# A float64-weight MoE kernel: one VectorE merge per weight block with its low bits from ScalarE, and late attention scores whose odd heads swap their two halves

## The chip, the cores and the metric

The kernel runs on one core of one Trainium2 chip. The metric is device time in microseconds (us) of one execution, the median of a few runs; lower is better. TensorE is PE in the profile (PEld its weight loads), VectorE is DVE, ScalarE is ACT, GpSimd is POOL, and SyncE (SP) issues every DMA.

## The reference

Three stages follow each other; batch 4, 8 heads of 48, 768 positions, model width 384.

```python
def _attn_ref(r, k, v, w, u):            # a recurrent state per head, decayed by w at every position
    for t in range(S):
        cur = np.einsum('bhd,bhe->bhde', u[None] * kt, vt)
        y[:, :, t] = np.einsum('bhd,bhde->bhe', rt, state + cur)
        state = wt[:, :, :, None] * state + np.einsum('bhd,bhe->bhde', kt, vt)

def _moe_ref(x, w_gate, w_val, w_out, rms_g):      # 3072 tokens, 384 -> 1536 -> 384
    xn = x / np.sqrt(np.mean(x * x, axis=-1, keepdims=True) + 1e-06) * rms_g
    g = xn @ w_gate
    return g * (1.0 / (1.0 + np.exp(-g))) * (xn @ w_val) @ w_out

def _moe2_ref(x, w_in, w_out, s, b):               # 3072 tokens, 384 -> 2048 -> 384
    r = np.maximum(x @ w_in, 0.0)
    return (s * (r * r) + b) @ w_out
```

The weights of both MoE stages are float64 and are handed over as 64-bit patterns.

## The kernel before, in words

**Work and order.** The 768 positions are 6 chunks of 128, and a chunk of all 4 batches is 512 columns. A pair `jb` (0 to 23) is one chunk of one batch. For each pair `attention` (L335) makes the decays, the scores, the output and the new state; `attention_x` normalises and turns the result; the first MoE (12 blocks f a chunk) and the second (16 blocks a chunk) follow. Every matmul of the MoE parts is done in three passes (high weight with high input, high with low, low with high; L629 to L631, L646). Chunks 0 and 1 are done in two parts, since not all weights are there yet, and partly in halves of 256 columns.

Nothing is issued in the order in which it is written. `op` hands each step to `Plan` with a due time and a cost per engine; `Plan.issue` walks through time with these costs and puts each step into its engine's queue, and `FIRST_OPS` (L53) replaces the due time of some 100 steps, found by their number. Where the planner sees TensorE idle, it puts in a filler, a matmul on zeros (`idle`, L820), which reads and writes nothing that is used. A step that may run on two engines (`BOTH`) goes to the one that is free first. The queues are in order: an engine that waits holds up all that stands behind.

**Weights** (`weights`, L576). A block of float64 weights comes in by DMA (`raw`, 768 or 384 numbers a row) and becomes a float32 pattern `pat` in three VectorE passes: L599 moves the high word three bits up, L603 merges the sign and exponent bits of the high word, L605 merges the top three bits of the low word. ScalarE then rounds `pat` to the high part of `w` (L610), and VectorE or, in the second MoE, either VectorE or GpSimd subtracts it for the low part (L620). There are 40 such pieces: 24 in the first MoE (12 of 768 and 12 of 384) and 16 of 768 in the second. Two `raw` and two `pat` buffers take turns.

**Scores** (`scores`, L399 to L405). Heads lie in two groups of 64 rows (`p`), four heads `h` each. From pair 4 on the scores of a head are done in two halves: keys 0 to 63 against 128 queries into the lower 64 output partitions, and keys 64 to 127 against the last 64 queries into the upper 64. So one quarter of the array streams 128 columns and the other 64, for each of the four heads. ScalarE copies the scores to `a` (L319), GpSimd zeroes what lies in the future with one select of 128x512 per `p` (L426), and TensorE multiplies by `v` in `sums` (L454) behind the products with the state (L445).

**Decays.** r and k are multiplied by running products of w (`re`, `ke`): on VectorE up to pair 11, from pair 12 on VectorE or GpSimd.

**Check.** Beside the second MoE, VectorE tests that all weights lie where the bit moves are right (`check_weight`, L760); otherwise a slow path, which does not run here, would do everything again.

## Time and profile before

| what | value |
|---|---|
| median of 3 runs | 967.43 us (966.9 to 967.6) |
| the profiled execution, own time | 967.64 us |
| its span, first to last instruction | 965.9 us |
| around the span | 1.7 us |
| busy share of the span: PE, DVE, ACT, POOL | 99%, 66%, 39%, 17% |
| granted TensorE clock, mean | 0.997 |

A line of a group of instructions gives source line, engine, operation, out<-in, shapes and count, then busy time, the mean of one in ns, the engine's idle time just before them and what ended most of it. In a timeline the first two numbers are start and length in us, and x32 says that 32 equal instructions were merged. Lengths of neighbours overlap a little, since an instruction starts before its predecessor has drained; the step from one start to the next is what an engine spends. A busy TensorE includes the fillers (L822).

### The profile page before, as it was taken

The page shows a single profiled execution, that of the slowest core. Times are in us where ns is not written, and L with a number is a line of the kernel's source. Part 1 is how long each engine was busy: PE and PEld are TensorE (multiplying, and loading weights), DVE is VectorE, ACT ScalarE, POOL GpSimd, SP SyncE. Part 2 cuts the span into 40 slices and gives each one's busy share as a digit, 9 for nine tenths or more (in the row PEclk, how much of TensorE's full clock was granted, in tenths as well). Part 3 has the DMA queues.
Part 4 walks back from the last instruction along what each step waited for, and adds up shares of the span by engine and source line. Part 5 has one row for each costly group of instructions (what it writes and reads, how often), then busy time and mean ns, then how long its engine had stood idle before and what let it go on. Part 6 is the DMA issues. An engine that isn't in the chain of part 4 may idle for free.

```text
span 965.9 us, 16522 instructions
## 1 busy us (share of the span) xinstructions
PE 952.9 (99%) x6585; PEld 788.7 (82%) x6589; DVE 635.2 (66%) x1051; ACT 378.8 (39%) x782; POOL 162.6 (17%) x211
## 2 busy tenths in 40 slices
PE   9999999999999999999999999999999999999996
PEld 5898998888888887888888878888888888888885
DVE  8999898547445445532588799987777874433332
ACT  4756545534323332332343353343433433433333
POOL 1212211255433323110025440000000000000000
PEclk9999999999999999999999999999999999999998
DMA  8655554245434443222466465553354530000001
GB/s 259 196 169 158 173 158 140 83 112 149 101 84 118 122 93 95 69 69 61 122 225 206 150 212 178 158 194 113 114 182 132 178 117 1 33 0 1 34 1 36
DMA packets 74422, 115.79 MB, mean 120 GB/s; under 512 B 28384, under 2 KB 48096, under 8 KB 74336
## 3 DMA queue, kind: packets, MB, share of 16 engines
q1 hardware_dynamic: 74336, 114.65, 39.6%
q8 instruction: 53, 0.87, 0.4%
q14 instruction: 33, 0.27, 0.1%
HBM read 99.16 MB, written 15.47 MB: 119 GB/s over the span
## 4 chain that ended last, share of the span: by engine, by line
PE 91%; DVE 5%; DMA 2%; ACT 1%; issue 1%; SPq 0%; POOL 0%; DVEq 0%
PE b L646 48%; PE b L629 12%; PE b L630 11%; PE b L631 11%; PE b L454 2%; PE b L404 2%; PE b L445 1%; DMA raw<-in_w 1%; DMA in<-in_rkw 1%; DVE pat L605 1%; DVE pat L603 1%; PE b L408 0%; PE b L822 0%; PE b L469 0%; DVE pat L599 0%
## 5 line engine op out<-in xcount | busy, mean ns | idle before, releaser
L646 PE MATMUL b<-xh,w 128*128 128x512 f32 (+1 forms) x1566 | 485.2, 374 | 0.9 <-DVE sg L316 0.6
L646 PEld LDWEIGHTS b<-xh,w 128*128 128x128 f32 x1566 | 287.7, 188 | 55.6 <-issue 1.9
L646 PE MATMUL b<-xl,w 128*128 128x512 f32 (+1 forms) x783 | 291.1, 372 | 0.0
L629 PE MATMUL b<-hh,w 128*128 128x512 f32 (+1 forms) x537 | 205.0, 382 | 1.1 <-ACT in L681 0.7
L630 PE MATMUL b<-hl,w 128*128 128x512 f32 (+1 forms) x537 | 202.5, 377 | 1.4 <-DVE hl L316 1.4
L631 PE MATMUL b<-hh,w 128*128 128x512 f32 (+1 forms) x537 | 202.1, 376 | 0.0
L319 ACT ACTIVATE sg<-b 128x512 f32<-128x512 f32 (+1 forms) x179 | 102.6, 573 | 249.1 <-PE b L646 245.0
L646 PEld LDWEIGHTS b<-xl,w 128*128 128x128 f32 x783 | 147.3, 188 | 25.4
L717 DVE SCALAR_TENSOR_TENSOR sg<-sg,cs,b 128x512 f32<-128x512 f32 (+1 forms) x97 | 71.9, 741 | 90.0 <-ACT sg L319 89.8
L630 PEld LDWEIGHTS b<-hl,w 128*128 128x128 f32 x537 | 101.0, 188 | 20.2 <-DVE hl L316 2.5
L629 PEld LDWEIGHTS b<-hh,w 128*128 128x128 f32 x537 | 101.0, 188 | 20.1 <-ACT in L681 0.9
L631 PEld LDWEIGHTS b<-hh,w 128*128 128x128 f32 x537 | 101.0, 188 | 18.5
L720 DVE SCALAR_TENSOR_TENSOR hl<-sg,cs,hh 128x512 fp32r<-128x512 f32 (+1 forms) x97 | 73.0, 753 | 43.4 <-ACT hh L319 43.2
L319 ACT ACTIVATE hh<-sg,cs 128x512 fp32r<-128x512 f32 (+1 forms) x97 | 70.1, 722 | 75.9 <-DVE sg L717 71.4
L319 ACT ACTIVATE hh<-sg 128x512 fp32r<-128x512 f32 (+1 forms) x82 | 47.6, 581 | 114.9 <-DVE sg L316 109.5
L316 DVE TENSOR_TENSOR sg<-b,sg 128x512 f32<-128x512 f32 (+1 forms) x82 | 51.0, 623 | 62.1 <-PE b L646 52.9
L316 DVE TENSOR_TENSOR hl<-sg,hh 128x512 fp32r<-128x512 f32 (+1 forms) x82 | 57.3, 698 | 18.2 <-ACT hh L319 17.5
L620 POOL TENSOR_TENSOR w<-pat,w 128x384 fp32r<-128x384 f32 x29 | 39.8, 1394 | 67.2 <-ACT w L610 67.2
L610 ACT ACTIVATE w<-pat 128x384 fp32r<-128x384 f32 x68 | 32.8, 520 | 37.5 <-DVE pat L605 37.3
L316 DVE TENSOR_TENSOR ys<-b,av 128x192 f32<-128x192 f32 x40 | 13.8, 351 | 47.8 <-PE b L454 47.8
L426 POOL TENSOR_SCALAR_AFFINE_SELECT a<-a 128x512 f32<-128x512 f32 x38 | 29.6, 796 | 85.7 <-ACT a L319 85.4
L603 DVE SCALAR_TENSOR_TENSOR pat<-raw,pat 128x768 uint32<-128x768 uint32 (+1 forms) x40 | 35.7, 894 | 0.0
(128 smaller groups left out, 843.4 us busy)
## 6 DMA issues: line engine op xcount, KB each, us to landing
raw<-in_w SPq DMA_DIRECT2D x56, 768.0 KB, 4.4
in<-in_rkw SPq DMA_DIRECT2D x24, 448.0 KB, 4.6
raw<-in_w SPq DMA_DIRECT2D x24, 384.0 KB, 3.6
n<-in_nat SPq DMA_DIRECT2D x18, 384.0 KB, 3.4
in<-in_rkw SPq DMA_DIRECT2D x24, 226.6 KB, 3.0
x2d<-o SPq DMA_DIRECT2D x21, 256.0 KB, 2.4
a<-in_rkw SPq DMA_DIRECT2D x24, 224.0 KB, 2.9
v<-in_nat SPq DMA_DIRECT2D x24, 192.0 KB, 4.0
```

The lines of the kernel that those rows point to most:

```text
L316: op(when, {e: cost[e] for e in engines}, lambda e: E[e].tensor_tensor(dst, a, b, f), reads, writes, port)
L319: op(when, {"act": act(n)}, lambda e: nc.scalar.activation(dst, src, func, **kw), reads, writes)
L426: op(t, {"pool": 0.60}, lambda e, s=A[p]: nc.gpsimd.affine_select(out=AT[s], in_=AT[s], compare_op=ALU.is_gt, fill=0.0, base=0, pattern=[[ ...
L603: op(t, {"dve": vec2(N)}, lambda e, word=word, pat=pat: nc.vector.scalar_tensor_tensor(pat(), word(1), 0xC0000000, pat(), ALU.bitwise_and, ...
L610: op(t, {"act": act(DM)}, lambda e, c=c, s=s, pat=pat: nc.scalar.activation(W[s][:, 0], pat(c).bitcast(F32), AF.Copy), [("pat", pi)], [("w ...
L620: op(t, {"dve": vec2(DM)} if ph == 0 else {"dve": vec2(DM), "pool": gps(DM)}, lambda e, c=c, s=s, pat=pat: E[e].tensor_tensor(W[s][:, 1], ...
L629: nc.tensor.matmul(dst, wt[:, 0, cols], xh, start=first, stop=False, skip_group_check=True)
L630: nc.tensor.matmul(dst, wt[:, 0, cols], xl, start=False, stop=False, skip_group_check=True)
L631: nc.tensor.matmul(dst, wt[:, 1, cols], xh, start=False, stop=last, skip_group_check=True)
L646: nc.tensor.matmul(dst, W[s][:, w, kk * 128:(kk + 1) * 128], xx[x][:, kk, sl], start=first and j == kk == 0, stop=last and kk == KD - 1 an ...
L717: op(t, {"dve": vec2(n)}, lambda e: nc.vector.scalar_tensor_tensor(sg, sg, s_col, p, ALU.mult, ALU.mult), [("ps", i)], [("sg", q)], False)
L720: op(t, {"dve": vec2(n)}, lambda e: nc.vector.scalar_tensor_tensor(hl, sg, b_col, hh.bitcast(F32), ALU.add, ALU.subtract), [("sg", q), ("h ...
```

## The change

**Weights.** Of the three VectorE passes two remain: the first now makes a constant with the sign bit (L616 after the change), the last shifts the high word by three and merges it with an exclusive or (L628). The three low bits are written between them by ScalarE: it reads one byte of each float64, scales it by 1/32 and writes it as the lowest byte of `pat` (L624). This needs weights under 2.0, and the check changes accordingly (a minimum in place of a masked product).

**Late pairs** (12 to 23). In odd heads the two halves go to the other half of the output partitions, so that each quarter of the array streams 128 columns for two heads and 64 for the other two. The rows of `a` of these heads are then swapped, so their `v` is loaded once more with its halves swapped (`vs`, two DMAs of 48 KB a pair in pieces of 384 bytes), and GpSimd's one select becomes three smaller ones per `p`. The products of r and k with their decays are on VectorE alone.

**Order.** The table `FIRST_OPS` is another one (its numbers count the new steps), so all queues are ordered anew. One line of it stands for all.

```diff
-TD, LATE = 3, 60
+TD, LATE, EVEN = 3, 60, 12
 FIRST_OPS = {
-    0: 281.6, 22: 529.2, 37: 729.3, 38: 985.1, 39: 488.5, 46: 298.9, 57: 804.2, 58: 733.2, 64: 673.4, 75: -711.3,
...
+    0: 36.2, 10: 196.1, 29: 1237.4, 37: 2075.4, 38: 1931, 39: -101.4, 41: -1180.2, 42: 822.5, 44: -295.5, 46: 2565.9,
...
+    VS = tiles(2, "vs", [128, HP, D])
-        ke, re, ne = (DVE, DVE, DVE) if jb < EARLY else (BOTH, BOTH, BOTH)
+        ke, re, ne = (DVE, DVE, DVE) if jb < EARLY else (DVE, DVE, BOTH)
+        if even:
+            for z in (0, 64):
+                dma(tl[3], VS[q][z:z + 64].rearrange("p (g x) d -> p g (x d)", g=2),
+                    nat[jb, 64 - z:128 - z, 0:DM].rearrange("t (g o m) -> t g o m", g=2, o=2)[:, :, 1],
+                    64 * 4 * D * 4, (), [("vs", q, z)])
+                    to = slice(64 - c0, C - c0) if even and h % 2 else cols
-                        nc.tensor.matmul(sc[p][cols, h, c0:], k[rows, h, cols], r[rows, h, c0:],
+                        nc.tensor.matmul(sc[p][to, h, c0:], k[rows, h, cols], r[rows, h, c0:],
-            op(t, {"pool": 0.60}, lambda e, s=A[p]: nc.gpsimd.affine_select(
-                out=AT[s], in_=AT[s], compare_op=ALU.is_gt, fill=0.0, base=0, pattern=[[0, HP], [1, C]],
-                channel_multiplier=-1), (), [("a", A[p])])
+            pairs = AT[A[p]].rearrange("p (g o) t -> p g o t", o=2)
+            keep(t, pairs[:, :, 0], 0.37, 0, 2)
+            keep(t, pairs[0:64, :, 1], 0.37, -64, 2)
+            keep(t, pairs[64:128, :, 1, 0:64], 0.25, 0, 2)
+                    vj = VS[q][:, j // 4 * 2 + p] if even and h % 2 else v[:, j, :]
-                    nc.vector.tensor_scalar(pat(), m, 3, 0x3FFFFFFF, ALU.logical_shift_left, ALU.bitwise_and)
+                    nc.vector.tensor_scalar(pat(), m, 0x80000000, 0xC0000000, ALU.bitwise_and, ALU.bitwise_xor)
-            op(t, {"dve": vec2(N)}, lambda e, word=word, pat=pat: nc.vector.scalar_tensor_tensor(
-                pat(), word(1), 0xC0000000, pat(), ALU.bitwise_and, ALU.bitwise_or), [("raw", ri)], [("pat", pi)])
-            op(t, {"dve": vec2(N)}, lambda e, word=word, pat=pat: nc.vector.scalar_tensor_tensor(
-                pat(), word(0), 29, pat(), ALU.logical_shift_right, ALU.bitwise_or), [("raw", ri)], [("pat", pi)])
+                op(t, {"act": act(N)}, lambda e, raw=raw, pat=pat: nc.scalar.activation(
+                    pat().bitcast(U8).rearrange("p (n four) -> p n four", four=4)[:, :, 0],
+                    raw.bitcast(U8).rearrange("p (n eight) -> p n eight", eight=8)[:, :, 3],
+                    AF.Copy, scale=1.0 / 32.0, bias=-31.0 / 64.0), [("raw", ri)], [("pat", pi)])
+                op(t, {"dve": vec2(N)}, lambda e, word=word, pat=pat: nc.vector.scalar_tensor_tensor(
+                    pat(), word(1), 3, pat(), ALU.logical_shift_left, ALU.bitwise_xor), [("raw", ri)], [("pat", pi)])
```

How the queues change is shown at three places. The numbers behind the names tell buffers apart; they are shifted by two after the change, since two tiles were added.

First place: TensorE, just after the first MoE matmuls have begun, around the turning of the fourth pair's output (L563, L580 after the change: `b<-cs,l`). Before:

```order
L822 LDWEIGHTS zero_115
L822 MATMUL b_157<-zero_115 128x256
L563 MATMUL b_160<-cs_63,l_109 128x128 x3
L822 LDWEIGHTS zero_115
L822 MATMUL b_157<-zero_115 128x256
L646 MATMUL b_157<-xh_116,w_79 128x256
L646 MATMUL b_157<-xl_118,w_79 128x256
```

After the change:

```order
L669 MATMUL b_158<-xl_118,w_81 128x256
L669 MATMUL b_158<-xh_116,w_81 128x256
L580 MATMUL b_162<-cs_63,l_109 128x128 x3
L652 MATMUL b_160<-hh_122,w_77 128x256
L653 MATMUL b_160<-hl_124,w_77 128x256
L654 MATMUL b_160<-hh_122,w_77 128x256
L652 MATMUL b_161<-hh_122,w_77 128x256
```

The fillers here are gone, and the turn stands behind the third weight column `w_81` where it stood behind the first part of `w_79`. In the whole queue 15 fillers of 256 columns become 3, and of the fillers of 512 columns 46 become 44 (20 of them at the very start in both).

Second place: VectorE, the first block of weights, among the first two pairs (`a_136`, `a_137`, `a_138`, `l_110`: their masked scores). Before:

```order
L599 TENSOR_SCALAR pat_114<-raw_112 128x384
L599 TENSOR_SCALAR pat_113<-raw_111 128x768
L603 SCALAR_TENSOR_TENSOR pat_114<-raw_112,pat_114 128x384
L316 TENSOR_TENSOR n_132<-in_128 112x512
L605 SCALAR_TENSOR_TENSOR pat_114<-raw_112,pat_114 128x384
L603 SCALAR_TENSOR_TENSOR pat_113<-raw_111,pat_113 128x768
L316 TENSOR_TENSOR l_110<-b_162,mk_153 128x512
L605 SCALAR_TENSOR_TENSOR pat_113<-raw_111,pat_113 128x768
```

After the change:

```order
L616 TENSOR_SCALAR pat_114<-raw_112 128x384
L368 RECIPROCAL rg_70<-l_105 112x4x8
L317 TENSOR_TENSOR in_129<-in_129,l_105 112x512
L317 TENSOR_TENSOR a_138<-b_163,mk_155 128x512
L317 TENSOR_TENSOR a_139<-b_164,mk_155 128x512
L370 SCALAR_TENSOR_TENSOR l_106<-in_129,rg_70 112x516
L317 TENSOR_TENSOR st_71<-b_161,pm_146 112x192
L317 TENSOR_TENSOR in_129<-in_129,l_106 112x512
L616 TENSOR_SCALAR pat_113<-raw_111 128x768
L628 SCALAR_TENSOR_TENSOR pat_114<-raw_112,pat_114 128x384
L317 TENSOR_TENSOR n_134<-in_128 112x512
L628 SCALAR_TENSOR_TENSOR pat_113<-raw_111,pat_113 128x768
```

One pass per piece is gone. Between the first pass and the merge of the piece of 384 stand eight other steps, and of the piece of 768 two.

Third place: ScalarE at the same time (`kt`, `ac`, `av` belong to the first pair). Before:

```order
L319 ACTIVATE minus<-cs_63 128x128
L319 ACTIVATE kt_135<-b_163 128x448
L319 ACTIVATE ac_146<-b_163 128x8
L549 ACTIVATE av_140<-v_130,ac_146 128x48 x8
L610 ACTIVATE w_77<-pat_114 128x384
```

After the change:

```order
L320 ACTIVATE minus<-cs_63 128x128
L624 ACTIVATE pat_114<-raw_112 128x384
L320 ACTIVATE kt_137<-b_165 128x448
L320 ACTIVATE ac_148<-b_165 128x8
L566 ACTIVATE av_142<-v_130,ac_148 128x48 x8
L624 ACTIVATE pat_113<-raw_111 128x768
L633 ACTIVATE w_77<-pat_114 128x384
```

The two byte steps stand ahead of the first pair's `kt` and behind its eight scalings.

In the late pairs the matmuls of 512 columns that stand on TensorE between a pair's scores and its products with the state change too: before 12 in ten of the twelve pairs (18 in pair 12, 15 in one more), after 27 in pairs 12 to 18 and then 18, 18, 15, 18, 18.

## Rows read from the trace of the kernel before

**Rows 1.** The page's part 1: busy us, share of the span, instructions.

```profile
PE 952.9 (99%) x6585; PEld 788.7 (82%) x6589; DVE 635.2 (66%) x1051; ACT 378.8 (39%) x782; POOL 162.6 (17%) x211
```

**Rows 2.** Windows: stretch, length, busy PE, PEld, DVE, ACT, POOL, PEclk, DMA share, GB/s.

```profile
24.00:48.00 24.00, 23.17 (x291) 19.64 (x295) 23.23 (x47) 17.12 (x56) 5.47 (x9) 1.00 0.64 199
...
260.00:540.00 280.00, 279.60 (x2136) 227.93 (x2135) 151.93 (x222) 93.18 (x176) 78.06 (x92) 1.00 0.41 117
...
572.00:966.00 394.00, 386.67 (x1722) 320.19 (x1720) 250.04 (x412) 141.67 (x226) 1.75 (x2) 0.99 0.29 94
```

**Rows 3.** Waits of PE: us in total, times, longest.

```profile
PE b L630 <- DVE hl L316: 1.4, 3, 0.7
...
PE b L646 <- DVE sg L316: 0.6, 1, 0.6
```

**Rows 4.** Timeline of PE in late pairs: state products, outputs; scores, the matmul behind them.

```profile
354.92 0.68 PE L445 MATMUL b<-st,in 48*64 48x48 f32 x32
355.53 1.14 PE L454 MATMUL b<-v,a 128*64 128x48 f32 x32
...
373.64 1.10 PE L404 MATMUL b<-in 48*64 48x128 f32 x32
374.67 0.50 PE L646 MATMUL b<-xh,w 128*128 128x512 f32 x1
```

**Rows 5.** Timeline of PE: first, dearest and last of nine stretches with short fillers.

```profile
35.15 0.28 PE L822 MATMUL b<-zero 128*128 128x256 bf16 x1
35.36 0.61 PE L469 MATMUL b<-v,l 128*64 128x48 f32 x15
...
50.74 0.61 PE L822 MATMUL b<-zero 128*128 128x256 bf16 x4
51.69 0.39 PE L629 MATMUL b<-hh,w 128*128 128x256 f32 x1 [0.33 <-DVE xl L571]
...
65.40 0.28 PE L822 MATMUL b<-zero 128*128 128x256 bf16 x1
65.44 0.36 PE L646 MATMUL b<-xh,w 128*128 128x256 f32 x1
```

**Rows 6.** The chain of waits in the second MoE: start, us, nine matmuls of 512 columns.

```profile
584.35 2.04 PE b L646 x9
```

**Rows 7.** Timeline from 30 to 32 us: the fourth pair's last decay product and scores.

```profile
30.19 0.69 DVE L316 TENSOR_TENSOR in<-in,l 112x512 f32<-112x512 f32 x1
30.79 0.95 DVE L605 SCALAR_TENSOR_TENSOR pat<-raw,pat 128x768 uint32<-128x768 uint32 x1
31.33 1.16 PE L404 MATMUL b<-in 48*128 48x128 f32 x16
31.66 0.35 DVE L571 SCALAR_TENSOR_TENSOR xl<-b,cs,xh 128x128 fp32r<-128x128 f32 x1
```

**Rows 8.** Timeline of DVE and PE: waits for GpSimd, for VectorE and for a DMA, a long pass.

```profile
367.08 1.85 DVE L357 TENSOR_TENSOR_SCAN eb<-in,ones 112x516 f32<-112x516 f32 x1 [0.48 <-POOL in L316]
...
369.56 0.50 PE L630 MATMUL b<-hl,w 128*128 128x512 f32 x1 [0.40 <-DVE hl L316]
...
555.09 0.56 DVE L599 TENSOR_SCALAR pat<-raw 128x768 uint32<-128x768 uint32 x1 [2.89 <-DMA raw<-in_w]
...
567.26 1.76 DVE L605 SCALAR_TENSOR_TENSOR pat<-raw,pat 128x768 uint32<-128x768 uint32 x1
```

**Rows 9.** Groups of ACT over the span, by shape.

```profile
L610 ACT ACTIVATE w<-pat 128x384 fp32r<-128x384 f32 x68 | 32.8, 520 | 37.5 <-DVE pat L605 37.3
...
L319 ACT ACTIVATE xh<-b,cs 128x128 fp32r<-128x128 f32 x36 | 11.8, 368 | 4.7 <-PE b L646 1.9 <-PE b L563 1.5 <-DVE xl L571 1.3
```

**Rows 10.** The page's part 6: DMA issues, count, KB each, median us to landing.

```profile
v<-in_nat SPq DMA_DIRECT2D x24, 192.0 KB, 4.0
...
raw<-kd SPq DMA_DIRECT2D x32, 64.0 KB, 2.7
```

**Rows 11.** Groups of POOL from 258 to 540 us: the select.

```profile
L426 POOL TENSOR_SCALAR_AFFINE_SELECT a<-a 128x512 f32<-128x512 f32 x20 | 13.3, 686 | 51.6 <-ACT a L319 51.5
```

More of the change, by code (lines that the diff above doesn't have):

```diff
@@ L13 @@
 U32 = mybir.dt.uint32
+U8 = mybir.dt.uint8
 I32 = mybir.dt.int32
@@ L414, in ac @@
                                  skip_group_check=True)
-        op(t, {"pe": 1.1 + 0.45 * (kp is not None)}, scores,
+        op(t, {"pe": (0.9 if even else 1.1) + 0.45 * (kp is not None)}, scores,
            [("k", q), ("r", q), "cs"] + [], [("ps", i) for i in i2] + ([] if kp is None else [("ps", i)]))
@@ L425, in attention, with keep @@
             cp(t, HP * C, AT[A[p]], sc[p], [("ps", i2[p])], [("a", A[p])])
-            op(t, {"pool": 0.60}, lambda e, s=A[p]: nc.gpsimd.affine_select(
-                out=AT[s], in_=AT[s], compare_op=ALU.is_gt, fill=0.0, base=0, pattern=[[0, HP], [1, C]],
-                channel_multiplier=-1), (), [("a", A[p])])
+            def keep(t, what, cost, base, n):
+                op(t, {"pool": cost}, lambda e, what=what: nc.gpsimd.affine_select(
+                    out=what, in_=what, compare_op=ALU.is_gt, fill=0.0, base=base, pattern=[[0, n], [1, what.shape[-1]]],
+                    channel_multiplier=-1), (), [("a", A[p])])
+            if not even:
+                keep(t, AT[A[p]], 0.60, 0, HP)
+                continue
+            pairs = AT[A[p]].rearrange("p (g o) t -> p g o t", o=2)
+            keep(t, pairs[:, :, 0], 0.37, 0, 2)
+            keep(t, pairs[0:64, :, 1], 0.37, -64, 2)
+            keep(t, pairs[64:128, :, 1, 0:64], 0.25, 0, 2)
         if kp is not None:
@@ L483, in attention @@
             op(t, {"pe": 1.5 + 0.6 * (not last)}, sums,
-               reads + [("r", q), ("v", q), ("st", b)] + tk * (not last),
+               reads + [("r", q), ("v", q), ("st", b)] + [("vs", q, z) for z in (0, 64)] * (jb >= EVEN - 2) + tk * (not last),
                [("ps", i) for i in iy] + ([] if last else [("ps", iu)]))
@@ L784, in run @@
             nc.vector.tensor_reduce(MX[:RW, 1:2], WR[1], AX.X, ALU.max)
[L785 removed]
+            ends = WS.rearrange("p (i two) -> p two i", two=2)
+            nc.vector.tensor_reduce(MX[:, 2:3], ends[:, 0], AX.X, ALU.max)
+            nc.vector.tensor_reduce(MX[:, 3:4], ends[:, 1], AX.X, ALU.min)
             nc.vector.tensor_scalar(MX[:, 0:1], MX[:, 0:1], W_LO, None, ALU.is_lt)
[L787 removed]
+            for col, lim, f in ((1, W_HI, ALU.is_gt), (2, W_BIG, ALU.is_ge), (3, W_TINY, ALU.is_lt)):
                 nc.vector.scalar_tensor_tensor(
[L789 removed]
+                    MX[:, 0:1], MX[:, col:col + 1], lim, MX[:, 0:1], f, ALU.max)
         op(t, {"dve": 1.0}, run, [("wr", jb, i) for jb in range(NJ) for i in range(2)] +
```

23 lines of the change are left out of this document (10 added, 13 removed), and 31 rows, old and new, of the table FIRST_OPS.

## Prediction

> **What bounds the kernel now.** I read four views in this order. The page's busy shares come first: TensorE is busy for 952.9 of 965.9 us [rows 1], so time can only go by giving TensorE less to do, or by removing its waits and the fillers, which count as busy. The windows show where another engine is full at the same time: VectorE works for 23.23 of the 24 us from 24 to 48, but for 152 of 280 us in the late pairs; ScalarE for 17.12 of the 24 and 93 of the 280 [rows 2]. So VectorE sets the pace of the start, and TensorE alone that of the late pairs and of the second MoE. The list of TensorE's waits is short, and its dearest lines are `hl` and `sg` from VectorE, 2.0 us together [rows 3]. Last come timelines of TensorE, for what a pair's scores take [rows 4] and where the fillers are [rows 5]. The sum is made against the profiled execution, 967.64 us, 0.2 above the median of the runs; 1.7 us of it lie outside the span and stay.
>
> **Scores of the late pairs: on the path.** TensorE is full there, so what the scores lose is gained. They take from 373.64 to 374.67, 1.03 us [rows 4]. A matmul is issued as two passes here (16 matmuls, x32), so one quarter of the array streams 8 passes of 128 columns and its neighbour 8 of 64; after the change each streams 4 and 4, that is 768 columns in place of 1024. No row shows the balanced form. If the time goes with the columns of the fuller quarter, a pair saves a quarter of 1.03, 0.26 us. Part of it may not shrink: the state products, of the same count and in the same quarters but with 48 columns each, take from 354.92 to 355.53, 0.61 us [rows 4]. So 8 times 80 more columns cost 0.42 us, and 256 fewer save 0.17. I take 0.21, the middle, as both ends come from rows of the same kind. Twelve pairs: **-2.5 us** (ends -2.0 and -3.1). The Trainium skill, TensorEngine Tiling (Array Packing), section Tiling Modes, says that tiles operate independently and can load and multiply in parallel; by it the upper saving holds and this term would be -3.1. These rows bear out that the halves overlap, not by how much.
>
> **The start: VectorE's lead becomes fewer fillers.** Behind the first MoE matmul the timeline has 15 fillers of 256 columns in nine stretches. From the first filler of a stretch to the next useful matmul the first, the dearest and the last cost 0.21, 0.95 and 0.04 us [rows 5]; all nine cost 2.5. The new queue has three such fillers, in one place; by the 0.95 for four they cost up to 0.7, by the 0.21 for one 0.6, and less where nothing is late behind them. Two of the 26 long fillers of the start go too; at 512 columns I price each like a matmul of that size, 2.04 / 9 = 0.23 us [rows 6]. That is 2.5 - 0.6 + 0.5 = 2.4, if no wait takes their place. VectorE's queue says that more is possible. The fourth pair's last decay product starts at 30.19, its scores at 31.33 [rows 7]. Ahead of it in the new order fewer steps stand: gone are two passes of 768 (0.87 each, from 30.79 to 31.66) and one of 384 (about half, 0.45), two masks of 512 (0.60 each, as the product from 30.19 to 30.79) and two small steps (0.26 each, 0.35 less the 0.09 by which neighbours overlap) [rows 7]; a first pass of 384, under 0.45, has come in. That makes some 3.6 us. VectorE has no idle row there, so TensorE can begin up to 3.6 us earlier, and gains less where its own work already fills the stretch. I take **-2.8 us**, nearer to the fillers' end (ends -2.4 and -3.6).
>
> **Waits in the middle.** At 367.08 a scan on VectorE waits 0.48 us for GpSimd's decay product; `hl` comes late behind it, and TensorE waits 0.40 us at 369 and loses a little more in starting again [rows 8]. With both products on VectorE that wait is gone; they cost VectorE 0.60 us each [rows 7], covered by its 128 idle us: **-0.5 us** (0 to -0.6). The other 1.6 us of waits for `hl` and `sg` lie mostly where the second MoE begins, at 558 and 567, behind weight passes. There VectorE waits 2.89 us for a block to land, which the change does not touch, and a pass takes 1.76 us [rows 8] that needs 0.95 elsewhere [rows 7]. I take somewhat over half: **-1.0 us** (0 to -1.6). That pass is long while GpSimd subtracts weights. The Trainium skill, GPSIMD Engine Reference, section 1 (Specifications), says that GpSimd shares its SBUF interfaces with VectorE and that they contend where an instruction of VectorE has two SBUF inputs. The dropped merge is such a one; by that rule a drop here is worth up to the long pass, and this term would go to its end of -1.6.
>
> **The byte step: hidden, with a residue.** ScalarE gets 40 more instructions. Its rows give 368 ns for 128 numbers and 520 for 384 [rows 9], 0.6 ns a number, so 0.75 us for 768; bytes with gaps may cost twice as much a number, about 1.2 us, or no more than the 0.52 of 384. 28 x 0.75 + 12 x 0.52 = 27 us fit in ScalarE's idle 61% [rows 1]. But the step lies between two VectorE passes, and VectorE waits if it isn't done. For the first piece of 768 two steps cover it, a merge of 0.45 and a product of 0.60, which is enough for 0.75 and not for 1.2. I book **+0.5 us** (0 to +3, which is a quarter of a us at each of the first 12 merges).
>
> **At nothing.** The `vs` transfers (48 KB) go with `v`, which lands in 4.0 us; smaller pieces of 64 KB land in 2.7 [rows 10], and both are due 14 us ahead of the pair by the code. Three selects in place of one of 0.69 us [rows 11] cost at most 4 x 0.69 = 2.8 us more between scores and outputs; the order gives 15 more matmuls there in seven pairs, 3.4 us by 0.227 each [rows 6], and 3 to 6 in the last five. If that cover were missing, each pair would lose the rest. The check runs beside the second MoE, where VectorE idles for 144 of 394 us [rows 2].
>
> **Sum.** -2.5 - 2.8 - 0.5 - 1.0 + 0.5 = -6.3: 961.3 on the profiled execution's scale, **961.1 us** as a median. All good ends give 967.4 - 8.9 = 958.5, all bad ones 967.4 - 4.4 + 3 = 966.0.
>
> **Rivals.**
> - The start gives nothing: the fillers go, but ScalarE's new place in the chain makes waits of the same size. For it: ScalarE is busy at 71% from 24 to 48 [rows 2]. Against it: eight steps cover the small piece's byte step. 961.1 + 2.8 = 963.9.
> - The halves share the array, and the scores take 1.03 us as before: 963.6. Against it: the fuller quarter alone explains most of the 1.03 by the slope above.
> - All good ends together: 958.5.
> - ScalarE becomes the bound of the start, and the kernel is slower. Place: the 12 merges up to 75 us, behind byte steps that queue on ScalarE. Price: each us that VectorE waits there is lost, since it has none idle. Without the booked 0.5 the gain is 6.8, so it decides from 6.8 / 12 = 0.57 us a merge; at 1.2 us a step and half a us of queue, less the cover, a merge waits about 0.8, 9.6 in all: 967.4 - 6.8 + 9.6 = 970.2. Against it: ScalarE still idles 7 of 24 us.
> - `vs` lands late, and the outputs of 12 pairs wait. It decides at a landing of 14 us, five times what small pieces take now [rows 10]; 1 us a pair beyond that gives 973.1. The Trainium skill, DMA: Bandwidth & Descriptors, section Specifications, puts the least transfer for full rate at 512 bytes, with a read and rewrite below; these pieces have 384. No row shows that rewrite as a long landing.
> - The order only moves waits: all but the scores' term cancel with new waits like that at 369, and half of the scores' too: about 966.2.
>
> **How the numbers follow.** The forecast has 0.60 (its own range 959 to 963.2), the start without gain 0.17, shared halves 0.05, all good ends 0.05, ScalarE as the bound 0.07, `vs` late 0.02, only moved 0.04. A measurement tells 0.2%, 1.9 us, from nothing, so faster means under 965.5: 0.60 + 0.05 + 0.05 and 0.15 of the 0.17 (its bytes at their dear end fall outside) make 0.85; same 0.07; slower 0.08. The range 958.5 to 965.5 leaves out the last three, half of the good ends and the tails of the start without gain, 0.17 in all.
>
> **What would show it.** Right: scores of a late pair in about 0.8 us; the first MoE matmul 1 to 2 us earlier and one stretch of short fillers; no wait for GpSimd's `in`; byte steps near 0.75 us with few VectorE waits for them. Wrong: merges that wait for the byte step and hand that on to TensorE, or late pairs that wait for selects or `vs`.

## The result and the profile after: slower by 1.3%

The changed kernel takes 980.64 us (median of four runs, 979.02 to 983.77), against 967.51 us for the kernel before beside it: the ratio is 1.0133, 95% interval 1.0111 to 1.0154. Thirteen us were added where 6.3 were forecast to go. The profiled execution has 979.02 us and a span of 977.3 us.

Part 1 of the page answers to [rows 1]:

```profile
PE 955.2 (98%) x6571; PEld 790.6 (81%) x6575; DVE 612.5 (63%) x994; ACT 409.6 (42%) x823; POOL 136.0 (14%) x236
```

The span grew by 11.4 us. TensorE's busy time grew by 2.3 of them, and its idle time by the other 9.1 (977.3 - 955.2 = 22.1, before 965.9 - 952.9 = 13.0). VectorE lost 22.7 us of work, as planned, but TensorE now waits for VectorE more than before. The list of TensorE's waits, to be held against [rows 3]:

```profile
PE b L669 <- DVE sg L317: 10.3, 8, 2.4
PE b L844 <- DVE col L824: 1.3, 1, 1.3
PE b L415 <- DMA cs<-in_cst: 1.2, 1, 1.2
...
PE b L653 <- DVE hl L317: 0.4, 1, 0.4
```

The wait for `sg` was 0.6 us once and is now 10.3 us in eight places, seven of them (8.0 us) between 230 and 395 us, in the late pairs. Each of these seven stands behind the same step of VectorE, as the next lines show for one of them. Three lines of what VectorE itself waits for over the span, those for loads and for the byte step (its waits for TensorE and ScalarE within the chain of the MoE are longer, as in the kernel before, and cost nothing):

```profile
DVE in L317 <- DMA in<-in_rkw: 28.3, 12, 3.6
...
DVE pat L616 <- DMA raw<-in_w: 8.5, 8, 3.9
...
DVE pat L628 <- ACT pat L624: 4.5, 6, 2.1
```

The dearest is the wait of the decay products for `in`, the next pair's block of r, k and w; before, it came to 9.7 us. One late pair shows how it reaches TensorE. The timeline of VectorE and then of TensorE (a bracket gives the idle time ahead of an instruction and what ended it):

```profile
377.29 0.58 DVE L539 STREAM_TRANSPOSE pat<-xg 128x384 f32<-128x384 f32 x1 [2.62 <-ACT xg L320]
381.47 1.93 DVE L317 TENSOR_TENSOR in<-in,eb 112x512 f32<-112x512 f32 x2 [3.60 <-DMA in<-in_rkw]
383.32 0.68 DVE L317 TENSOR_TENSOR sg<-b,sg 128x512 f32<-128x512 f32 x1
...
384.05 0.50 PE L669 MATMUL b<-xh,w 128*128 128x512 f32 x1 [1.80 <-DVE sg L317]
```

The chain of waits for the same stretch shows the same path as the one that sets the end:

```profile
376.85 4.60 DMA in<-in_rkw
381.45 0.02 issue
381.47 1.93 DVE in L317 x2
383.40 0.61 DVE sg L317
384.01 0.04 issue
384.05 0.96 PE b L669 x3
```

The block of `in` is under way for 4.60 us. VectorE has nothing to do from 377.87 on, but the two products stand at the head of its queue, and `sg`, which needs only what TensorE and ScalarE have long done, stands behind them. TensorE runs out of work 1.80 us before `sg` is there. The windows over the late pairs answer to the middle one of [rows 2]: TensorE was busy for all but 0.4 of 280 us, and is now idle for 6.8.

```profile
260.00:540.00 280.00, 273.21 (x2104) 221.58 (x2103) 151.93 (x230) 98.11 (x180) 63.01 (x115) 0.99 0.43 120
```

The queues themselves tell where this comes from, and no time is needed to read it. VectorE's queue at a late pair in the order of the instructions, before:

```
L522 STREAM_TRANSPOSE pat0_113<-xg0_139 128x3x4x32
L316 TENSOR_TENSOR sg1_121<-b1_157,sg1_121 128x512
L316 TENSOR_TENSOR hl1_125<-sg1_121,hh1_123 128x512
L316 TENSOR_TENSOR in0_128<-in0_128,eb1_134 112x512
L316 TENSOR_TENSOR sg0_120<-b1_157,sg0_120 128x512
```

and after the change:

```
L539 STREAM_TRANSPOSE pat0_113<-xg0_141 128x3x4x32
L317 TENSOR_TENSOR in0_128<-in0_128,eb0_135 112x512
L317 TENSOR_TENSOR in0_128<-in0_128,eb1_136 112x512
L317 TENSOR_TENSOR sg0_120<-b1_159,sg0_120 128x512
...
L317 TENSOR_TENSOR hl0_124<-sg0_120,hh0_122 128x512
```

Before, one `sg` and one `hl` stood between the transposition and the (single) product, and the other product was GpSimd's, where nobody stands behind it. Now both products come first. It is so in seven of the twelve late pairs, and these seven have the waits for `sg`.

Where the time was lost is read from the start of the n-th matmul of the MoE parts, as its delay in us against the kernel before (worked out from the traces; in the kernel before #400 starts at 112 us, #700 at 164, #920 at 231, #1500 at 389, #2100 at 537). Some attention matmuls may lie on the other side of such a mark, so single entries are good to some 2 us; the last column is the end.

| kernel | first | #400 | #700 | #920 | #1500 | #2100 | last |
|---|---|---|---|---|---|---|---|
| after | +3.4 | +0.5 | +5.2 | +5.0 | +14.5 | +13.7 | +11.4 |
| after, second profile (g4) | +3.1 | +3.7 | +5.8 | +5.6 | +18.0 | +17.2 | +14.8 |
| e2, products on GpSimd | +1.4 | +2.8 | +4.6 | +4.5 | +6.8 | +6.0 | +3.6 |
| e3, products held back | +3.2 | +3.8 | +9.3 | +9.1 | +12.8 | +13.3 | +10.9 |
| e7, both parts, old order | +0.7 | +3.0 | +3.1 | +2.9 | +1.2 | +0.4 | +0.2 |
| g1, old table | -0.5 | +10.4 | +14.5 | +16.0 | +29.7 | +29.9 | +27.5 |
| g5, old table, either engine | -0.6 | +6.3 | +11.0 | +11.5 | +12.7 | +12.3 | +9.9 |
| g3, bytes in the second MoE | +0.2 | -0.2 | -0.2 | -0.4 | -0.1 | -1.0 | -0.9 |
| h3, products ahead | +0.3 | 0.0 | 0.0 | +8.8 | +47.8 | +57.6 | +57.0 |

In the changed kernel 9.5 us are lost between #920 and #1500, which is the first of the two stretches of late pairs, and 0.5 to 5 come and go ahead of it. After #1500 it gains 0.8 us to #2100 and 2.3 from there to the end, so its +11.4 is 5.0 + 9.5 - 0.8 - 2.3.

### The profile page after: what moved, and what is told of

It is laid out like the page before. It is cut to its first block, busy times and chain, and to the rows that moved or that the text cites. A ratio compares the mean times of both kernels' runs of the same rounds, so it can differ in the third digit from the quotient of the medians.

```text
span 977.3 us, 16545 instructions
## 1 busy us (share of the span) xinstructions
PE 955.2 (98%) x6571; PEld 790.6 (81%) x6575; DVE 612.5 (63%) x994; ACT 409.6 (42%) x823; POOL 136.0 (14%) x236
## 4 chain that ended last, share of the span: by engine, by line
PE 87%; DMA 6%; DVE 3%; SPq 2%; issue 1%; ACT 0%; DVEq 0%
PE b L669 46%; PE b L652 11%; PE b L653 11%; PE b L654 11%; DMA in<-in_rkw 3%; PE b L471 2%; PE b L411 2%; SPq L311 2%; DVE in L317 1%; PE b L461 1%; DMA raw<-in_w 1%; DMA v<-in_nat 1%; DMA cs<-in_cst 1%; PE b L841 1%; DVE sg L317 1%
## 5 line engine op out<-in xcount | busy, mean ns | idle before, releaser
L669 PE MATMUL b<-xh,w 128*128 128x512 f32 (+1 forms) x1566 | 490.1, 377 | 10.3 <-DVE sg L317 10.3
L317 DVE TENSOR_TENSOR hl<-sg,hh 128x512 fp32r<-128x512 f32 (+1 forms) x82 | 51.8, 632 | 25.7 <-ACT hh L320 25.2
L794 DVE TENSOR_REDUCE ws<-pat 128x1 f32<-128x768 f32 (+1 forms) x80 | 64.4, 826 | 0.7
L434 POOL TENSOR_SCALAR_AFFINE_SELECT a<-a 128x256 f32<-128x256 f32 (+3 forms) x86 | 39.3, 477 | 95.4 <-ACT a L320 93.9
L317 DVE TENSOR_TENSOR in<-in,eb 112x512 f32<-112x512 f32 x40 | 32.3, 829 | 28.3 <-DMA in<-in_rkw 28.3
L624 ACT ACTIVATE pat<-raw 128x768 uint8<-128x768 uint8 (+1 forms) x40 | 37.9, 951 | 12.4 <-DVE pat L616 12.2
L643 POOL TENSOR_TENSOR w<-pat,w 128x384 fp32r<-128x384 f32 x30 | 33.7, 1140 | 61.0 <-ACT w L633 61.0
```

The lines of the kernel that those rows point to most:

```text
L317: op(when, {e: cost[e] for e in engines}, lambda e: E[e].tensor_tensor(dst, a, b, f), reads, writes, port)
L434: op(t, {"pool": cost}, lambda e, what=what: nc.gpsimd.affine_select(out=what, in_=what, compare_op=ALU.is_gt, fill=0.0, base=base, patter ...
L624: op(t, {"act": act(N)}, lambda e, raw=raw, pat=pat: nc.scalar.activation(pat().bitcast(U8).rearrange("p (n four) -> p n four", four=4)[:, ...
L643: op(t, {"dve": vec2(DM)} if ph == 0 else {"dve": vec2(DM), "pool": gps(DM)}, lambda e, c=c, s=s, pat=pat: E[e].tensor_tensor(W[s][:, 1], ...
L669: nc.tensor.matmul(dst, W[s][:, w, kk * 128:(kk + 1) * 128], xx[x][:, kk, sl], start=first and j == kk == 0, stop=last and kk == KD - 1 an ...
L794: op(t, {"dve": vec2(n)}, lambda e, j=j, fn=fn: nc.vector.tensor_reduce(WS[:, 2 * i + j:2 * i + j + 1], mag.bitcast(F32), AX.X, fn), [("pa ...
```

## The experiments

Every kernel was timed in five rounds beside the kernel before. The groups ran on different chips, where the kernel before took 967.2 to 968.0 us, so a ratio says more than a difference of medians. The changed kernel itself, once more (g4), ran from 975.5 to 983.8 us, so 2 or 3 us between two kernels in the new order may be nothing. "Old order" is the sequence that the table of the kernel before gives to all queues.

| run | what it is | median us | ratio to before, 95% interval |
|---|---|---|---|
| e5 | before + swapped halves, old order | 966.52 | 0.9984 [0.9970, 0.9997] |
| e6 | before + byte step, old order | 970.41 | 1.0028 [1.0014, 1.0041] |
| e7 | before + both, old order | 968.31 | 1.0011 [0.9994, 1.0029] |
| e4 | after, halves as before | 983.85 | 1.0161 [1.0139, 1.0183] |
| e9 | after, three VectorE passes | 993.66 | 1.0288 [1.0258, 1.0319] |
| e2 | after, late products on GpSimd | 972.90 | 1.0060 [1.0046, 1.0074] |
| e3 | after, late products held back | 975.29 | 1.0065 [1.0048, 1.0082] |
| e12 | after, one product on each engine | 979.70 | 1.0135 [1.0108, 1.0163] |
| e1 | after, first ten DMAs as before | 983.42 | 1.0179 [1.0157, 1.0201] |
| e10 | e1, first small piece later | 984.36 | 1.0167 [1.0142, 1.0192] |
| e11 | after, one piece later | 981.50 | 1.0133 [1.0108, 1.0158] |
| e13 | e10, e11 and e12 together | 981.18 | 1.0128 [1.0100, 1.0155] |
| g4 | after again | 979.94 | 1.0105 [1.0072, 1.0138] |
| g1 | after with the old table | 991.99 | 1.0241 [1.0204, 1.0279] |
| g5 | g1, products on either engine | 979.63 | 1.0132 [1.0095, 1.0169] |
| g3 | e5 + byte step in the second MoE | 965.99 | 0.9967 [0.9950, 0.9983] |
| h2 | g3, both products on VectorE | 967.28 | 0.9999 [0.9985, 1.0013] |
| h3 | h2, products ahead of `sg` | 1020.64 | 1.0547 [1.0533, 1.0562] |

### The parts, one at a time (e5, e6, e7, e4, e9)

The parts were put into the kernel before without moving anything: the `vs` loads and the three selects are issued inside the steps of `v` and of the one select, and the byte step takes the place of the second pass (`...` stands for lines that are not shown).

```diff
+                    to = slice(64 - c0, C - c0) if even and h % 2 else cols
-                        nc.tensor.matmul(sc[p][cols, h, c0:], k[rows, h, cols], r[rows, h, c0:],
+                        nc.tensor.matmul(sc[p][to, h, c0:], k[rows, h, cols], r[rows, h, c0:],
...
-            op(t, {"dve": vec2(N)}, lambda e, word=word, pat=pat: nc.vector.scalar_tensor_tensor(
+                op(t, {"dve": vec2(N)}, lambda e, raw=raw, pat=pat: nc.scalar.activation(
...
```

e5 has the first two lines, e6 the last, e7 both. e4 and e9 go the other way: the changed kernel with the old halves (no `vs`, one select), and with the old three passes in the same places of the queues.

> The kernel before, in its own order, with the late pairs' swapped halves alone (vs transfers right behind v, three selects where one stood). Theory 'places': the balanced scores pay 12 x 0.2 us: 967.5 - 2.4 = 965.1. Theory 'parts': the added transfers and selects take that back or more: 967.5 or above.

> The kernel before, in its own order, with the weights' byte step on ScalarE in the slot of the second VectorE pass (so two VectorE passes in place of three). The step takes 1.08 us for 768 and 0.63 for 384 in the changed kernel. Theory 'places': VectorE loses 30 us of work, half of it in the first 150 us where it is full; the fillers stay in the program, so the gain is small: 965 to 967. Theory 'parts': the merges of the start wait for the byte step, 12 x 0.5 us or more, and hand it on: 970 to 974.

> Both parts in the old order. Theory 'places': the sum of the two, 963 to 965, faster than the kernel before by 0.3 to 0.4%. Theory 'parts': slower than the kernel before.

> The changed kernel in the same order with the scores of the late pairs in the old halves: no vs transfers, one select in place of three, v in the sums. Theory 'places': the scores' 12 x 0.2 us come back and nothing else: 980.6 + 2.4 = 983.0. Theory 'parts': the vs transfers and selects cost more than the balanced scores save, so it is faster than 980.6.

> The changed kernel in its own order, with the weights made by three VectorE passes again: the pass stands where the byte step stood. Theory 'places': 30 us come back to VectorE, some 16 of them before 150 us, where it has about 10 us idle; the time rises by 3 to 8 us, 984 to 989. Theory 'parts': without the wait for ScalarE it falls below 980.6.

Against what was expected, e4 came out as 'places' said and e6 as 'parts' did. e5 lies between the two, e7 can't be told from the kernel before, and e9 lost more than 'places' said. The halves gain 1.5 us alone (e5; 0.3 to 2.9 by its interval), and 3.2 are lost when they are taken back from the changed kernel (e4 against after). In e5's timeline of TensorE the scores of a late pair take from 374.10 to 374.93, 0.83 us, where [rows 4] have 1.03:

```profile
374.10 0.90 PE L413 MATMUL b<-in 48*64 48x128 f32 x32
374.93 0.50 PE L662 MATMUL b<-xh,w 128*128 128x512 f32 x1
```

The byte step costs 2.5 us in the old order (e6; 1.4 to 4.0 by its interval) and 1.8 on top of the halves (e7 against e5). It costs them at the start: e7 is 3.0 us late at #400 and loses nothing after that. VectorE's waits for ScalarE from 0 to 75 us, which were 0.8 us in the kernel before, are 7.6 in e7:

```profile
DVE xl L588 <- ACT xh L322: 4.3, 5, 1.4
DVE w L643 <- ACT w L633: 2.3, 2, 1.9
...
DVE pat L628 <- ACT pat L624: 1.0, 2, 0.5
```

VectorE seldom waits for the byte step itself; it waits for ScalarE's other work, the rounding of `x` and `w`, which stands behind the byte steps in ScalarE's queue. In the changed order the same step is a gain: without it (e9) the kernel is 13 us slower still. So neither of these two parts explains the loss: in the old order both together end within 0.2% of the kernel before.

### The late products (e2, e3, e12)

Three ways to place the products of the late pairs. e2 issues both decay products of late pairs on GpSimd, from the places that they have in the plan. e3 leaves them on VectorE and holds them back until the next `sg` and `hl` have gone into the queue. e12 has r's product on GpSimd and k's on VectorE behind `sg` and `hl`.

```diff
-        op(when, {e: cost[e] for e in engines}, lambda e: E[e].tensor_tensor(dst, a, b, f), reads, writes, port)
+        op(when, {e: cost[e] for e in engines}, lambda e: E[on or e].tensor_tensor(dst, a, b, f), reads, writes, port)
...
-        tt(t, re, HP * C, r, r, ET[:, :, 0:C], ALU.mult, [ek], [("r", q)])
...
+        tt(t, re, HP * C, r, r, ET[:, :, 0:C], ALU.mult, [ek], [("r", q)], "pool" if jb >= EARLY else None)
...
```

> The changed kernel in the same order, with both decay products of the late pairs (jb 12 and up) emitted on GpSimd. Theory 'places': TensorE's 10.3 us of waits for sg come from VectorE, which stands in front of these products until the block of in has landed (28.3 us of waits); on GpSimd that wait blocks nobody, the waits for sg fall under 2 us, and the time falls by 8 to 10 us, to 971 or 972. Theory 'parts': the waits at the late pairs come from the vs transfers and the three selects, which stay; the time falls by at most 2 us, and GpSimd, with two more products of 1.7 us in a pair, may make it worse.

> The changed kernel with the decay products of the late pairs still on VectorE alone, but behind the next sg and hl in its queue, as the kernel before had its one product there; what depends on them moves with them. If the place in the queue is what costs (theory 'places'), this gains as much as GpSimd does: 8 to 10 us, 971 or 972, with few waits for sg. If it is the engine (two products of 0.6 us are too much for VectorE there), it gains little, under 3 us. Theory 'parts': 980.

> The changed kernel with one decay product of each late pair (r) emitted on GpSimd in its place, and the other (k) left on VectorE but behind the next sg and hl, as in the kernel before. Theory 'places': no queue with work for TensorE stands in front of the block of in; better than both e2 (972.9) and e3 (975.3), where VectorE's transposes waited for GpSimd, or two products stood together: 970 to 972. Rival (the place matters, the engine not): as e3, 975.

e2 gains 7.7 us and e3 5.3, less than the 8 to 10 expected, and both gain it in the late pairs: from #920 to #1500 they lose 2.3 and 3.7 us where the changed kernel loses 9.5. In e2 the list of TensorE's waits has changed places, from `sg` to `hl`:

```profile
PE b L653 <- DVE hl L317: 4.5, 6, 1.5
PE b L669 <- DVE sg L317: 1.7, 1, 1.7
```

VectorE's transposition of `in` (L527) now waits 14.7 us for GpSimd's products, with `hl` behind it. e12 missed its 970 to 972: its waits for `in` fall from 28.3 to 2.4 us, but one wait of 4.7 us has come in at 244 us, and the time is the changed kernel's.

```profile
PE b L674 <- ACT hh L340: 4.7, 1, 4.7
```

There ScalarE's copy of an output block waits 7.32 us for the DMA that frees its buffer, which SyncE issues behind another that waits. So in e12 one wait of the fixed order was mended and another took its place.

### The start (e1, e10, e11, e13)

e1 issues the first ten DMAs in the sequence of the kernel before. e10 adds that the first small piece's field and byte steps stand behind the large piece's. e11 puts off, by the same means, the piece whose load stops VectorE at 136 us for 3.92 us. e13 is e10, e11 and e12 in one; the last line below is e13's, with the moves of e10 and e11.

```diff
         assert len(order) >= n
+        lead = [(i, "sp") for i in (8, 9, 10, 44, 45, 0, 1, 46, 80, 90)]
+        order = lead + [x for x in order if x not in lead]
+        until = {91: 81, 665: 627}
...
```

> The changed kernel with the first ten transfers issued in the sequence that the kernel before has (the first pair's v third, the constants ahead of the first weight pieces); nothing else moves. Theory 'places' (the new order puts transfers and instructions where they wait; the parts themselves pay): the constants land before 9.6 us instead of 10.98, TensorE does not fall idle at 7.7 to 11 us, the granted clock stays at 1.00 from 12 to 18 us, and the first MoE matmul starts near 34 us in place of 37.3. At the end this is worth between 0.5 us (what was left of it at the 400th MoE matmul) and 3.4 us: 977 to 980. Theory 'parts' (the byte step on ScalarE and the swapped halves cost more than they save, wherever they stand): the start stays late behind merges, and the time stays at 980.6.

> As e1 (the first transfers in the old sequence), and the first VectorE pass of the first small weight piece, with its byte step on ScalarE, moved behind the large piece's pass: in e1 VectorE stood 2.43 us in front of that piece's transfer, the byte step stood ahead of kt on ScalarE, and TensorE waited 2.1 us for kt. Theory 'places' (an instruction stands in its queue in front of a transfer that has not landed, and the queue behind it stands too): no such wait is left, TensorE is not idle for long before 20 us, the granted clock stays at 1.00 at least to 18 us, and the first MoE matmul starts near 34 us. Gain against e1 about 5 us (978), against the changed kernel 2 to 4 us (977 to 979). Rival (the byte step itself is too slow for the start, wherever it stands): the first MoE matmul stays past 36.5 us, and the time at 980 or more.

> The changed kernel with one instruction moved, and its byte step with it: the first pass of the eleventh large weight piece (at 136.22 us, behind 3.92 us of waiting for its transfer) goes five places down VectorE's queue, behind the sg and hl that stood behind it. Theory 'places': TensorE's wait of 2.35 us for sg at 137 goes, and the time falls by 1.5 to 2.5 us (978 to 979). Rival (the stretch is short of transfers: TensorE needs that weight soon, whatever VectorE's order): the wait moves on, and the time stays within 0.5 us of the changed kernel.

> The three moves of e10, e11 and e12 together in the changed kernel: nothing of the change's parts is undone but one product of a late pair. Theory 'places': the gains add, 980.6 - (2 to 4) - (1.5 to 2.5) - (8 to 10) = 964 to 969, that is, level with the kernel before or below it. Rival (the parts cost too): it stays over 970.

All four missed their gains, and by their numbers e10 and e13 came out as their rivals said. In e1 the blocks of `in` come earlier, and then VectorE waits for the first piece of weights, which is loaded later; ScalarE's byte step stands ahead of `kt` and hands the wait on to TensorE, 2.15 us:

```profile
12.83 0.36 DVE L618 TENSOR_SCALAR pat<-raw 128x384 uint32<-128x384 uint32 x1 [2.43 <-DMA raw<-in_w]
13.23 0.63 ACT L626 ACTIVATE pat<-raw 128x384 uint8<-128x384 uint8 x1 [4.16 <-DVE pat L618]
13.73 0.52 ACT L322 ACTIVATE kt<-b 128x448 f32<-128x448 f32 x1
14.30 0.61 PE L488 MATMUL b<-v,kt 128*64 128x48 f32 x15 [2.15 <-ACT kt L322]
```

With that step out of the way (e10) the first MoE matmul still starts 2.4 us late. In e11 the wait at 137 us is gone, but TensorE's waits for `hl` grow from 0.4 to 3.1 us, and nothing was gained.

### The table (g4, g1, g5)

g4 is the changed kernel once more. g1 puts the table of the kernel before, number by number, into the changed one; g5 is g1 with the products open to either engine again.

```diff
-        ke, re, ne = (DVE, DVE, DVE) if jb < EARLY else (DVE, DVE, BOTH)
+        ke, re, ne = (DVE, DVE, DVE) if jb < EARLY else (BOTH, BOTH, BOTH)
```

> The changed kernel itself once more, beside the others on the same chip, so that differences of 2 us can be told: both theories expect 980.6, within 1.5.

> The changed kernel with one thing undone: the table FIRST_OPS of the kernel before, word for word (its numbers, up to 921, mean the same instructions in both kernels; the late pairs' lie above). Theory 'two causes': the new table makes the start and the stretch from 118 to 140 us 5 to 7 us dearer than the old one would, and the late pairs lose another 6 us because their two decay products, on VectorE alone, are put ahead of sg in its queue whatever the table; so this gives back the first part only: 973 to 976. Rival 'parts': the table is not to blame, the byte step is; 979 or more. Rival 'table alone': 968.

> As g1, and the late pairs' decay products open to both engines as in the kernel before (one of them then lands on GpSimd, and the other behind sg and hl in VectorE's queue). Theory 'two causes': both are gone, 967 to 969, level with the kernel before, as e7 was. Rival 'parts': 974 or more.

The new table isn't what costs: the old one is 12 us dearer in the changed kernel (g1 against g4). Its numbers, up to 921, name the same steps in both kernels, so that isn't why; what makes it dearer is not shown. g1 and g5 missed their forecasts, and by their numbers alone the rival 'parts' fits, but e5, e6 and e7 speak against it. What g5 against g1 shows is the products alone. Opened to both engines they give 12.4 us, and 12.5 between #920 and #1500 (13.7 - 1.2). g1's list of TensorE's waits begins with the same line as the changed kernel's, and g5's has no wait for VectorE's `sg`:

```profile
PE b L654 <- DVE sg L302: 10.9, 8, 2.1
```

### Place or engine, and a version that beats both (g3, h2, h3)

g3 is e5 with the byte step for the second MoE's weights only, where ScalarE has room. h2 takes g3 and issues the second product on VectorE too, at the place in the queue that it has. h3 is h2 with one difference, on VectorE's queue alone: the products of late pairs move ahead of the `sg` and `hl` that they stood behind.

```diff
+        for i in sorted(self.late):
+            at = [x[0] for x in order].index(i)
+            e = order.pop(at)[1]
+            steps = [n for n, x in enumerate(order[:at]) if x[0] in self.steps][-2:]
+            first = max([n for n, x in enumerate(order[:at]) if x[0] in self.deps[i]], default=-1) + 1
+            order.insert(max(steps[0], first), (i, e))
```

> The kernel before, in its own order, with the swapped halves of the late pairs (as e5), and the byte step for the second MoE's weights alone; the first MoE's keep their three VectorE passes. In e7 VectorE's waits for ScalarE in the first 75 us rose from 0.8 to 7.6 us, and TensorE was 2.6 us later at 70 us. If the byte step costs at the start alone, this is faster than e7 (968.3) by 2 to 3 us and than e5 (966.5) by up to 0.6: 965 to 966.5. If it costs wherever it stands: 967 or more.

> As g3_byte_late (966.0), with the second decay product of each late pair emitted on VectorE too, in the slot that GpSimd's had: both stand behind sg and hl in VectorE's queue, as the kernel before has its one. Theory 'place': the engine does not matter, 965.5 to 967. Rival 'engine' (two products on VectorE alone are too much there): 970 or more.

> As h2, with these products moved up in VectorE's queue to stand ahead of the sg and hl that they stood behind; no other queue changes by a row. Theory 'place': TensorE waits for sg again as in the changed kernel, and the time rises against h2 by 5 to 8 us, to 971 to 974: the loss is made out of this one thing. Rival 'engine', or something else of the new order: as h2, within 1.5 us.

g3 is faster than the kernel before by 0.33% (0.17 to 0.50) and than the changed one by 14 us (g4, on the same chip). h2 is within 0.2% of the kernel before. Its median is 1.3 us above g3's, but on another chip; by the ratios it is 0.3% slower, some 3 us, so which engine does the products matters little beside their place. g3 came out as forecast, and h2 0.3 us past its 'place' range. h3 moved the way that 'place' said, but by 53 us where 5 to 8 were forecast. A late pair of h2 on VectorE:

```profile
361.85 0.69 DVE L319 TENSOR_TENSOR sg<-b,sg 128x512 f32<-128x512 f32 x1
363.24 0.69 DVE L319 TENSOR_TENSOR hl<-sg,hh 128x512 fp32r<-128x512 f32 x1 [0.70 <-ACT hh L322]
365.66 1.30 DVE L319 TENSOR_TENSOR in<-in,eb 112x512 f32<-112x512 f32 x2 [1.72 <-DMA in<-in_rkw]
366.87 0.68 DVE L319 TENSOR_TENSOR sg<-b,sg 128x512 f32<-128x512 f32 x1
```

and one of h3, VectorE and then TensorE:

```profile
399.89 0.58 DVE L548 STREAM_TRANSPOSE pat<-xg 128x384 f32<-128x384 f32 x1 [2.29 <-ACT xg L329]
404.59 1.29 DVE L326 TENSOR_TENSOR in<-in,eb 112x512 f32<-112x512 f32 x2 [4.12 <-DMA in<-in_rkw]
405.80 0.69 DVE L326 TENSOR_TENSOR sg<-b,sg 128x512 f32<-128x512 f32 x1
...
406.54 0.50 PE L685 MATMUL b<-xh,w 128*128 128x512 f32 x1 [4.02 <-DVE sg L326]
```

In h2 the products wait for the same load, 1.72 us, and TensorE has `sg` and `hl` to go on with. In h3 TensorE waits 33.1 us for `sg` over the span. The rows are those of the changed kernel, so the mechanism is shown from both sides. Put in, it costs 53 us. Taken out, it gives 5 and 8 us in the new order (e3, e2) and 12 by the old table (g5 against g1), but nothing in e12, where another wait took its place. Why h3's nine waits are 3.7 us on average, and the changed kernel's seven 1.1, is not shown.

## Why the prediction was wrong

**The scores: right.** 388.36 to 389.19 us in the changed kernel is 0.83 us a pair; twelve times 0.20 is the -2.4 of the forecast's -2.5. End to end the halves alone gave 1.5 (e5).

```profile
388.36 0.90 PE L411 MATMUL b<-in 48*64 48x128 f32 x32
389.19 0.50 PE L669 MATMUL b<-xh,w 128*128 128x512 f32 x1
```

**The waits in the middle: the step that failed.** "With both products on VectorE that wait is gone; they cost VectorE 0.60 us each [rows 7], covered by its 128 idle us". The wait of 0.48 us for GpSimd did go. But an engine's idle time covers a moved step only if the step can run at its place in the queue. Before, GpSimd held the other product and could wait for the load at next to no cost (that 0.48 us); on VectorE, ahead of `sg`, the same wait for a load of 4.60 us is TensorE's. The price of 0.60 us each was too low as well: in six of the seven places the two products took 1.93 us, beside a product of GpSimd's (`av`), and 1.30 in the seventh. The term is not -0.5: from #920 to #1500 the changed kernel lost 9.5 us, 8.0 of them in the seven waits for `sg`, and e2 and e3 took back 7.2 and 5.8. The order of the instructions showed the danger before any run: both products directly behind the transposition, `sg` behind them.

**The start: wrong too.** -2.8 was booked and the first MoE matmul was to come 1 to 2 us earlier; it came at 37.65 us, 3.4 later than in the kernel before (34.25), with the fillers gone as forecast. "VectorE has no idle row there, so TensorE can begin up to 3.6 us earlier" took the old queue's fullness for the new one's. The fourth pair's scores, which were to move forward too, start 3.0 us later than the 31.33 of [rows 7]:

```profile
34.33 1.16 PE L411 MATMUL b<-in 48*128 48x128 f32 x16
```

The window from 0 to 24 us has VectorE busy for 18.02 us, where the kernel before had 20.96:

```profile
0.00:24.00 24.00, 20.01 (x155) 12.79 (x157) 18.02 (x31) 9.87 (x30) 3.52 (x16) 0.86 0.82 227
```

The 3 us taken off VectorE became idle time, behind loads and TensorE's state products (1.4 and 0.9 us of waits that the kernel before does not have there). What would mend it stays open. Seven profiles have the changed kernel's own start (after, g4, e2, e3, e4, e11, e12), and their first MoE matmul comes 0.8 to 3.4 us late; with e10's moves it is 2.4 late, and 0.5 in e13, which gains nothing by the end. Nor is the byte step's share settled: in the old order it makes TensorE 3.0 us late at #400 (e7), but without it the changed kernel starts 3.9 us late (e9).

**The phase boundary: better than booked.** TensorE has no wait for VectorE between 540 and 600 us, and gains 2.5 us from the 2100th to the 2300th MoE matmul, against -1.0 (0 to -1.6). VectorE's long pass stays long, 1.68 us at 570.11 beside GpSimd, as in [rows 8]; so the waits went though the pass stayed long.

**The byte step: its size off, its end about right.** It takes 1083 ns for 768 numbers and 644 for 384, not 750 and 520. The forecast's 0.6 ns a number came from two rows of different kinds (in [rows 9] the one of 128 numbers reads a second operand, `cs`). ScalarE's groups by shape:

```profile
L624 ACT ACTIVATE pat<-raw 128x768 uint8<-128x768 uint8 x28 | 30.3, 1083 | 8.9 <-DVE pat L616 8.7
...
L624 ACT ACTIVATE pat<-raw 128x384 uint8<-128x384 uint8 x12 | 7.7, 644 | 3.5 <-DVE pat L616 3.5
```

Its cost in the old order, 1.8 to 2.5 us, lies within the 0 to +3 of the forecast.

**At nothing: right in the new order.** No late pair of the changed kernel has TensorE waiting for `vs` (which lands in 2.8 us, the median) or a select, and e5 gains with both. But the cover that the prediction counted on belongs to the new order: in e5, by the old one, TensorE waits 1.6 us for the selects, in two late pairs, which can be why it gains 1.5 us and not 2.4.

```profile
PE b L469 <- POOL a L439: 1.6, 4, 0.9
```

**The rivals.** "The order only moves waits" named the right kind of cause, but held it to be neutral at worst, and "ScalarE becomes the bound" named an effect that e7 shows at 2 us, not as the cause of a loss. None put a price on a wait that moves onto an engine that feeds TensorE.

**What stays open.** Of the 9.5 us from #920 to #1500 the waits for `sg` are 8.0; the clock (0.99 in the window above, 1.00 before) can be part of the rest, and no run splits it. The 5.0 us lost ahead of #920, at the start and around a wait of 2.35 us for `sg` at 137 us, have no shown cause, and no run gave them back: e2, the fastest kernel in the new order, is still 0.6% slower than the kernel before.

## What to carry to other kernels

When work is moved onto an in-order engine, look in the order of the instructions for the load that it needs and for what stands behind it: idle time of an engine covers a step only where the step's input is there when its turn comes. A step that waits for a load belongs behind the steps that feed the busiest engine, or on an engine that nobody waits for. And before a part of a change is blamed, put it alone into the old order (e5, e6, e7): here each of the first two parts was worth within 0.3%, both products on VectorE cost 0.3% more (h2), and the new order with all three took 12 us more than the old one with the first two (after against e7).

## What the runs showed of the hardware

- **Bytes with gaps were dearer for ScalarE.** In the byte step 384 more numbers cost 1083 - 644 = 439 ns, 1.14 ns a number. Float32 numbers without gaps cost 0.86 in the same profile, (597 - 377) / 256:

```profile
L320 ACT ACTIVATE sg<-b 128x512 f32<-128x512 f32 x157 | 93.8, 597 | 215.9 <-PE b L669 214.7 <-DVE hl L317 0.8
...
L320 ACT ACTIVATE sg<-b 128x256 f32<-128x256 f32 x22 | 8.3, 377 | 9.5 <-PE b L669 7.1 <-DVE hl L317 2.1
```

  The Trainium skill, ScalarE: Activation LUTs, section What ACT_TABLE_LOAD costs, gives 186 ns and 0.833 ns an element for an ACTIVATE with immediate scale and bias, whatever the function, in fp32 and bf16; by it 768 take 826 ns and 384 take 506, both estimates. The row of `w`, 520 ns for 384, agrees; the byte step, one byte read of eight and one written of four, took some 30% more. No run tells the bytes from the gaps.
- **With VectorE and GpSimd both at work, one of them took longer.** Two products of a late pair took VectorE 1.93 us in six of the seven places, and GpSimd's `av` beside them 0.84 to 1.01 us. In the seventh the products took 1.30 us and `av` 1.39:

```profile
309.87 1.30 DVE L317 TENSOR_TENSOR in<-in,eb 112x512 f32<-112x512 f32 x2 [2.66 <-DMA in<-in_rkw]
310.47 1.39 POOL L317 TENSOR_TENSOR av<-v,ac 128x384 f32<-128x384 f32 x1 [4.85 <-DMA v<-in_nat]
...
381.91 0.94 POOL L317 TENSOR_TENSOR av<-v,ac 128x384 f32<-128x384 f32 x1 [5.63 <-DMA v<-in_nat]
```

- **TensorE's clock fell after an idle stretch.** In the changed kernel's profile it was granted 0.50 from 12 to 18 us (1.2 GHz in place of 2.4), after TensorE had been busy for 0.98 of the two us from 10 to 12; in the second profile of the same kernel (g4), busy for 2.00 of those two us, 1.00.

```profile
12.00:18.00 6.00, 5.63 (x58) 4.45 (x61) 5.12 (x10) 3.49 (x12) 0.28 (x2) 0.50 0.80 216
```

  The start was late by 3.1 us in the second profile as well, and by 0.8 and 1.8 us in e11 and e12, which have 1.00 there too; so the clock can be part of the lateness and isn't all of it. In h3, with its waits of up to 5.1 us for `sg`, the mean from 260 to 580 us is 0.94: by an estimate at most 0.06 of 320 us, some 19 us, come from the clock on top of the 33.1 of waits.

```profile
260.00:580.00 320.00, 286.89 (x2097) 230.54 (x2096) 138.07 (x213) 92.72 (x172) 64.05 (x118) 0.94 0.35 97
```
